# Moving the start addresses of SBUF tiles to multiples of 2 KB in a three-stage fp32 kernel

## The chip, the cores and the metric

The kernel runs on one core of a Trainium2 chip. The metric is the device time of one execution in microseconds, as the median of several runs. Beside it stands one profiled execution, from which every row below is taken.

## The reference, cut to what matters

Three stages follow each other. `q`, `k` and `v` are (8, 8, 576, 64), and positions attend to each other within chunks of 64 (`q_c`, `k_c`, `v_c`). The first network goes from 512 to 1024 columns twice, then to 1024 and back to 512; the second from 512 to 2048 and back. Everything is float32 and the result is (4608, 512).

```python
def _attn_ref(q, k, v):
    ...
    scores = scale * np.matmul(q_c, k_c.transpose(0, 1, 2, 4, 3))
    scores = scores - np.max(scores, axis=-1, keepdims=True)
    attn = np.exp(scores)
    attn = attn / (np.sum(attn, axis=-1, keepdims=True) + 1e-09)
    out = np.matmul(attn, v_c)
    ...

def _moe_ref(x, w1, w2, w3, w_out):
    a = x @ w1
    b = x @ w2
    h = a * b @ w3
    return (h @ w_out).astype(np.float32)

def _moe2_ref(x, w_in, w_out, alpha):
    h = x @ w_in
    g = np.maximum(h, 0.0) + alpha * np.minimum(h, 0.0)
    return (g @ w_out).astype(np.float32)
```

## The kernel before

**Arithmetic.** Each float32 operand of the large products is split into a high and a low half in a format that TensorE takes in one pass (`F32R`, four bytes an element), and a product is made of three matmuls: high with low, high with high, low with high (`PASSES`, line 24; `mm3`, lines 209 to 211). Each of these has 128x128 weights and 512 moving columns. The weights `w3` and `w_out` of the first network are multiplied with each other once at the start (`fold`, tile `wc`), so that the first network is two projections (`proj1`, tiles `a` and `b`), their product, and one projection through `wc` (`proj_wc`, accumulators `acc`). The second network is `proj2` and `proj_out`.

**Tiles in SBUF.** Four kinds matter here.
- *Granules* (`granule`, line 118): 32 slots of 4 KB in a partition, each two rows of 512 float32. They hold, one after another in time, `qk`, `v` and `e` of the attention, the weights `wa` and `wo`, the folded `wc`, and later the second network's `w2` (`w` in the profile). All matmuls but those of `fold` and `proj_out` take their weights from a granule; `fold` and `proj_out` take their moving rows from one.
- *x* (line 311, and line 382 for the second network, where the tile is `y`): two buffers of 16 KB, high and low half of 512 tokens. They are moving rows of `proj1` and `proj2`.
- *Halves of g* (`halves`, line 115, tag `gs`): three buffers of 4 KB. They are moving rows of `proj_wc` and weights of `proj_out`; `fold` takes its weights (`w3`) from them.
- *Temporaries*: `raw` (3 of 4 KB), `tmp` (8 of 2 KB: `m`, `p`, `a`, `g`, `y`, `o`), `pt` (4 KB), and small ones: `mx` and `sm` (64 bytes each, two buffers) and `warm` (4 bytes).

Pools are laid one after another in a partition and tags within a pool in the order of their first use, each rounded up to 32 bytes and no more. `const` holds `ident` (512 bytes) and `alpha_sb` (64 bytes); `gran` follows, then `work`, in which `warm` comes first, then `raw`, `tmp`, `mx`, `sm`, `pt`, `x` and `gs`. So the small tiles decide where the large ones behind them begin. Within a granule, in x and in the halves of g, a moving row begins a whole number of 2 KB behind the tile's start, and a block of weights a whole number of 512 bytes.

**Order.** Up to about 230 us the kernel follows a list of steps written out by hand (`STARTUP`), in which the attention of the first three blocks, the splitting of the weights and `proj1` are interleaved. Then come three blocks of `proj_wc`, from stored products (`g_dram`), then six blocks of `proj1`, `product` and `proj_wc` with the attention of later blocks between them, and then nine blocks of `proj2` and `proj_out`. All DMAs are issued from SyncE's queue. TensorE runs what the loops give it in order; the InOrder helper (lines 91 to 105) records every instruction of the three engines, so that all of them stand under line 100 in the profile, and tiles tell them apart.

Of the kernel before, what the change touches and what calls it, by code (L numbers as in the profile page):

```python
# [10 lines left out]
F32 = mybir.dt.float32  # L11
F32R = mybir.dt.float32r
AF = mybir.ActivationFunctionType
# [4 lines left out]
P = 128  # L18
# [41 lines left out]
def tile_attention_moe_moe(ctx: ExitStack, tc: tile.TileContext, qkv: bass.AP, w12: bass.AP,  # L60
# [16 lines left out]
    NU = NT // (2 * P)  # L77

    const = ctx.enter_context(tc.tile_pool(name="const", bufs=1))
    gran = ctx.enter_context(tc.tile_pool(name="gran", bufs=1))  # L80
    work = ctx.enter_context(tc.tile_pool(name="work", bufs=2))
    psum = ctx.enter_context(tc.tile_pool(name="psum", bufs=1, space=bass.MemoryType.PSUM))

    ident = const.tile([P, P], F32, name="ident")
    make_identity(nc, ident)
    alpha_sb = const.tile([P, NF2], F32, name="alpha_sb")
    g_dram = {(b, f): tc.dram_tile([P, TB], F32, name=f"g_dram{b}_{f}") for b in range(LEAD) for f in range(NF1)}
    y_dram = [tc.dram_tile([P, KD, TB], F32, name=f"y_dram{b}") for b in range(NB)]
    w2_dram = {(f, h): tc.dram_tile([P, 2, TB], F32, name=f"w2_dram{f}_{h}") for f in range(NF2) for h in range(2)}
# [15 lines left out]
    pe, act, dve = InOrder(nc.tensor), InOrder(nc.scalar), InOrder(nc.vector)  # L105
# [112 lines left out]
    un = {}  # L218
# [41 lines left out]
                                         start=True, stop=True)  # L260

    def attn_max(u):
        mx = un[u]["mx"] = work.tile([P, 2, 8], F32, tag="mx", name="mx")
        dve.tensor_reduce(out=mx, in_=un[u]["s"].rearrange("p h (a k) -> p h a k", k=D), axis=AX.X, op=ALU.max)
        dve.tensor_scalar_mul(mx, mx, -SCALE)

    def attn_exp(u, tiles=range(2)):
        mx, s, e = un[u]["mx"], un[u]["s"], un[u]["e"]
        if tiles[0] == 0:
            un[u]["sm"] = work.tile([P, 2, 4, 2], F32, tag="sm", name="sm")  # L270
        sm = un[u]["sm"]
        for j in tiles:
            for a in range(4):
                for h2 in range(2):
                    n, h = 4 * j + a, h2 ^ (a & 1 if u >= CROSS else 0)
                    act.activation(out=e[:, j, a, h], in_=s[:, h2, n * D:(n + 1) * D], func=AF.Exp,
                                         bias=mx[:, h2, n:n + 1], scale=SCALE, accum_out=sm[:, j, a, h:h + 1])
# [128 lines left out]

    act.activation(out=work.tile([P, 1], F32, tag="warm", name="warm", bufs=1), in_=ident[:, 0:1], func=AF.Exp)
    for u in range(4):  # L410
        unit_tiles(u)
    for load, n in ((load_qk, 0), (convert_load, 0), (load_qk, 1), (load_v, 0), (convert_load, 1), (load_v, 1),
# [6 lines left out]
    for step in STARTUP.split():  # L419
# [4 lines left out]
        elif kind in "ABCDE":  # L424
            {"A": convert_a, "B": convert_b, "C": convert_c, "D": convert_d, "E": convert_e}[kind](n)
        elif kind in "ST":
            {"S": attn_scores, "T": attn_transpose}[kind](n, lent.get(n, "att"))
        elif kind in "MXYPV":
            {"M": attn_max, "X": attn_exp, "Y": attn_softmax, "P": attn_copy, "V": attn_values}[kind](n)
        elif kind in "cd":  # L430
            attn_out(n, kind == "d")
        elif kind == "a":
            if sets % 2:
                pp = pair("p01", "ab")
                ab[tuple(rest)] = [pp[:, 0], pp[:, 1], None]
            else:
                ab[tuple(rest)] = [bank("a"), bank("b"), None]
            sets += 1
            proj1(*rest, 0, ab[tuple(rest)][0])
        elif kind == "k":  # L440
            a = ab[tuple(rest)][2] = tmp("a")
            act.copy(a, ab[tuple(rest)][0])
        elif kind == "b":
            proj1(*rest, 1, ab[tuple(rest)][1])
        elif kind == "m":
            _, ps, a = ab.pop(tuple(rest))
            product(*rest, a, ps)
        elif kind == "h":
            fold(*rest)
        elif kind in "sw":  # L450
            fold_split(n, kind == "w")
        elif kind == "g":
            load_g(*steps[n])


    def unit_steps(u, cut):


        def first():
            attn_scores(u)  # L460
            attn_max(u)
            attn_exp(u, range(1 if cut else 2))

        def second():
            if cut:
                attn_exp(u, range(1, 2))
            attn_softmax(u)
            if u + 1 < NU:
                load_unit(u + 1)

        def third():
            attn_transpose(u)
            attn_copy(u)

        def fourth():
            attn_values(u)
            attn_out(u, False)
            attn_out(u, True)
        return [first, second, third, fourth]
# [107 lines left out]
```

## Time and profile before

| | us |
|---|---|
| median of 3 runs | 1557.77 |
| lowest, highest | 1557.25, 1558.16 |
| the profiled execution | 1558.09 |
| its span, first to last instruction | 1556.3 |

The profiled execution is 0.3 us above the median, and 1.8 us of it lie outside the span. TensorE is busy for 98% of the span, VectorE for 51%, ScalarE for 27%; the chain of work that ended last is TensorE's for 95%. A busy TensorE is not TensorE at its peak, since matmuls are pipelined and each one's recorded length overlaps the next: what one costs is read from how far the starts of groups lie apart, not from the mean length.

### The profile page before, as it was taken

How to read it: one execution, taken by the hardware profiler on the slowest of the kernel's cores; microseconds unless marked ns; L12 is line 12 of the kernel's file. 1: busy time of each engine (PE TensorE's matmuls, PEld its weight loads, DVE VectorE, ACT ScalarE, POOL GpSimd, SP SyncE). 2: the span in 40 equal slices, each digit the busy share in tenths (PEclk: the TensorE clock that was granted, in tenths of full speed). 3: DMA queues.
4: the chain of work that ended last, by engine and by line, in shares of the span. 5: the costliest groups of instructions: out<-in, count | busy, mean ns of one | idle time of the engine just before them, and what ended most of it. 6: DMA issues, size and time to landing. Idle time of an engine off the chain costs nothing.

```text
span 1556.3 us, 21102 instructions
## 1 busy us (share of the span) xinstructions
PE 1530.3 (98%) x8688; PEld 1228.2 (79%) x8688; DVE 793.0 (51%) x1250; ACT 421.0 (27%) x1108; POOL 0.7 (0%) x6
## 2 busy tenths in 40 slices
PE   5999999999999999999999999999999999999998
PEld 5778877788888888888788888888888888888887
DVE  7988984376666663231434343443434344343433
ACT  6553335344444443321111111111111111111111
POOL 0000000000000000000000000000000000000000
PEclk9999999999999999999999999999999999999999
DMA  8544446354554544155301010010101000000000
GB/s 298 164 130 148 147 160 217 99 186 169 178 172 160 186 166 163 45 172 190 95 0 55 0 55 1 14 41 1 55 0 55 0 14 28 1 27 0 28 1 27
DMA packets 61712, 141.89 MB, mean 91 GB/s; under 512 B 6576, under 2 KB 20912, under 8 KB 61616
## 3 DMA queue, kind: packets, MB, share of 16 engines
q1 hardware_dynamic: 61616, 140.54, 27.1%
q8 instruction: 68, 1.11, 0.3%
q14 instruction: 28, 0.23, 0.0%
HBM read 98.57 MB, written 41.94 MB: 90 GB/s over the span
## 4 chain that ended last, share of the span: by engine, by line
PE 95%; DVE 2%; ACT 2%; DMA 1%; issue 0%; SPq 0%; ACTq 0%
PE acc L100 38%; PE b L100 24%; PE a L100 23%; PE ab L100 4%; PE wc L100 3%; PE pa L100 2%; PE sc L100 1%; ACT e L100 1%; DMA g<-g_dram 1%; DVE m L100 0%; DMA qk<-in_qkv 0%; DVE mx L100 0%; DVE p L100 0%; DVE e L100 0%; DVE x L100 0%
## 5 line engine op out<-in xcount | busy, mean ns | idle before, releaser
L100 PE MATMUL acc<-w,gs 128*128 128x512 f32 x1728 | 426.5, 396 | 0.0
L100 PEld LDWEIGHTS acc<-w,gs 128*128 128x128 f32 x1728 | 324.5, 188 | 78.8
L100 ACT CAST gs<-g 128x512 fp32r<-128x512 f32 x168 | 104.5, 622 | 683.2 <-DVE g L100 656.8
L100 PE MATMUL acc<-gs,wc 128*128 128x512 f32 x864 | 213.8, 398 | 2.1 <-DVE gs L100 2.1
L100 PE MATMUL b<-y,w 128*128 128x512 f32 x864 | 213.0, 395 | 0.0
L100 PE MATMUL a<-y,w 128*128 128x512 f32 x864 | 213.0, 395 | 0.0
L100 PEld LDWEIGHTS acc<-gs,wc 128*128 128x128 f32 x864 | 160.1, 187 | 43.4 <-DVE gs L100 3.4
L100 PEld LDWEIGHTS a<-y,w 128*128 128x128 f32 x864 | 162.0, 187 | 39.5
L100 PEld LDWEIGHTS b<-y,w 128*128 128x128 f32 x864 | 162.0, 187 | 39.5
L100 DVE TENSOR_TENSOR gs<-g,gs 128x512 fp32r<-128x512 f32 x168 | 116.3, 693 | 133.1 <-ACT gs L100 126.9
L100 PE MATMUL b<-x,wa 128*128 128x512 f32 x720 | 180.0, 398 | 0.1
L100 PE MATMUL a<-x,wa 128*128 128x512 f32 x720 | 178.1, 396 | 1.4 <-DVE x L100 1.4
L100 PEld LDWEIGHTS a<-x,wa 128*128 128x128 f32 x720 | 134.6, 187 | 34.5 <-DVE x L100 1.6
L100 PEld LDWEIGHTS b<-x,wa 128*128 128x128 f32 x720 | 133.3, 188 | 32.3 <-DVE wa L100 0.5
L100 DVE TENSOR_SCALAR g<-b,alpha_sb 128x512 f32<-128x512 f32 x72 | 54.0, 750 | 189.5 <-PE b L100 189.5
L100 DVE TENSOR_SCALAR g<-a,alpha_sb 128x512 f32<-128x512 f32 x72 | 54.0, 750 | 173.7 <-PE a L100 173.7
L100 DVE TENSOR_SCALAR m<-m 128x512 f32<-128x512 f32 (+1 forms) x144 | 60.9, 424 | 67.1 <-ACT m L100 65.7
L100 ACT ACTIVATE e<-sc,mx 128x64 f32<-128x64 f32 x288 | 85.7, 353 | 28.9 <-DVE mx L100 28.9
L100 DVE TENSOR_TENSOR a<-b,a 128x512 f32<-128x512 f32 x60 | 41.3, 689 | 93.3 <-PE b L100 82.5
L100 ACT COPY a<-a 128x512 f32<-128x512 f32 x60 | 35.9, 599 | 151.2 <-PE a L100 132.5
L100 PE MATMUL ab<-x,wa 128*128 128x512 f32 x288 | 71.1, 402 | 2.7 <-ACT a L100 2.7
L100 ACT ACTIVATION_READ_ACCUMULATOR e<-sc,mx 128x1 f32 x288 | 70.2, 247 | 0.0
(55 smaller groups left out, 982.2 us busy)
## 6 DMA issues: line engine op xcount, KB each, us to landing
qk<-in_qkv SPq DMA_DIRECT2D x36, 512.0 KB, 6.5
raw<-in_w2nd SPq DMA_DIRECT2D x32, 512.0 KB, 4.0
w_dram<-wm SPq DMA_DIRECT2D x32, 512.0 KB, 3.1
w<-w_dram SPq DMA_DIRECT2D x32, 512.0 KB, 3.3
y_dram<-y SPq DMA_DIRECT2D x36, 256.0 KB, 2.9
yraw<-y_dram SPq DMA_DIRECT2D x18, 512.0 KB, 4.2
out<-o SPq DMA_DIRECT2D x36, 256.0 KB, 2.1
raw<-in_w SPq DMA_DIRECT2D x16, 512.0 KB, 4.4
```

The lines of the kernel that those rows point to most:

```text
L100: ins = op(*args, **kw)
```

## The change

Only the places of tiles change. `mx` and `sm` move from the pool `work` to a pool of their own, `small`, with two buffers each as before; `warm` moves to `const`; and a tile of 1,056 bytes, `shift`, is laid down that nothing reads or writes. Starts in a partition, in bytes past a multiple of 2 KB:

| tiles | before | after |
|---|---|---|
| granules (32) | 704 | 0 |
| raw, tmp | 736 | 0 |
| pt, x, halves of g | 992 | 0 |
| mx, sm | 736 and 800, 864 and 928 | the same |
| ident | 128 | 128 |

Every engine gets the same instructions in the same order with the same waits on the same semaphores, before and after; only addresses differ. No tile shares a buffer with another than before, and the PSUM tiles stay where they are.

```diff
@@ -77,6 +77,8 @@
     const = ctx.enter_context(tc.tile_pool(name="const", bufs=1))
+    small = ctx.enter_context(tc.tile_pool(name="small", bufs=2))
+    shift = ctx.enter_context(tc.tile_pool(name="shift", bufs=1))
     gran = ctx.enter_context(tc.tile_pool(name="gran", bufs=1))
     work = ctx.enter_context(tc.tile_pool(name="work", bufs=2))
@@ -84,6 +86,8 @@
     alpha_sb = const.tile([P, NF2], F32, name="alpha_sb")
+
+    shift.tile([P, 264], F32, name="shift")
@@ -260,14 +264,14 @@
     def attn_max(u):
-        mx = un[u]["mx"] = work.tile([P, 2, 8], F32, tag="mx", name="mx")
+        mx = un[u]["mx"] = small.tile([P, 2, 8], F32, tag="mx", name="mx")
...
         if tiles[0] == 0:
-            un[u]["sm"] = work.tile([P, 2, 4, 2], F32, tag="sm", name="sm")
+            un[u]["sm"] = small.tile([P, 2, 4, 2], F32, tag="sm", name="sm")
@@ -406,7 +410,7 @@
-    act.activation(out=work.tile([P, 1], F32, tag="warm", name="warm", bufs=1), in_=ident[:, 0:1], func=AF.Exp)
+    act.activation(out=const.tile([P, 1], F32, name="warm"), in_=ident[:, 0:1], func=AF.Exp)
```

## Rows read from the trace of the kernel before

**Rows 1.** Page, part 1: busy us of each engine, share of the span, instructions.
```profile
PE 1530.3 (98%) x8688; PEld 1228.2 (79%) x8688; DVE 793.0 (51%) x1250; ACT 421.0 (27%) x1108; POOL 0.7 (0%) x6
```

**Rows 2.** Stretches: us, then PE, PEld, DVE, ACT, POOL, PEclk, DMA, GB/s.
```profile
20.00:290.00 270.00, 262.18 (x1876) 209.78 (x1877) 211.18 (x365) 120.05 (x340) 0.00 (x0) 0.99 0.52 166
290.00:742.00 452.00, 452.00 (x3209) 362.40 (x3207) 234.28 (x400) 173.30 (x520) 0.00 (x0) 1.00 0.47 158
742.00:1556.30 814.30, 809.66 (x3469) 650.68 (x3468) 336.55 (x468) 113.91 (x178) 0.00 (x0) 1.00 0.07 23
```

**Rows 3.** Groups by shape, TensorE: busy us, mean ns of one, idle before.
```profile
L100 PE MATMUL acc<-w,gs 128*128 128x512 f32 x1728 | 426.5, 396 | 0.0
L100 PEld LDWEIGHTS acc<-w,gs 128*128 128x128 f32 x1728 | 324.5, 188 | 78.8
L100 PE MATMUL acc<-gs,wc 128*128 128x512 f32 x864 | 213.8, 398 | 2.1 <-DVE gs L100 2.1
L100 PE MATMUL b<-y,w 128*128 128x512 f32 x864 | 213.0, 395 | 0.0
L100 PE MATMUL a<-y,w 128*128 128x512 f32 x864 | 213.0, 395 | 0.0
L100 PE MATMUL b<-x,wa 128*128 128x512 f32 x720 | 180.0, 398 | 0.1
L100 PE MATMUL a<-x,wa 128*128 128x512 f32 x720 | 178.1, 396 | 1.4 <-DVE x L100 1.4
...
L100 PE MATMUL ab<-x,wa 128*128 128x512 f32 x288 | 71.1, 402 | 2.7 <-ACT a L100 2.7
...
L100 PE MATMUL wc<-wo,w 128*128 128x512 f32 x192 | 45.6, 396 | 0.0
```

**Rows 4.** Chain of waits, whole span: start us, length us, engine, tile, count.
```profile
1.17 4.49 DMA qk<-in_qkv
...
162.87 11.20 PE wc L100 x48
...
188.08 5.60 PE ab L100 x24
```

**Rows 5.** Order of time, TensorE alone, 690 to 700 us.
```profile
691.65 2.96 PE L100 MATMUL a<-x,wa 128*128 128x512 f32 x12
694.45 2.96 PE L100 MATMUL b<-x,wa 128*128 128x512 f32 x12
```

**Rows 6.** Order of time, all engines, 900 to 912 us.
```profile
902.10 2.96 PE L100 MATMUL b<-y,w 128*128 128x512 f32 x12
904.67 2.75 PEld L100 LDWEIGHTS acc<-w,gs 128*128 128x128 f32 x12
904.90 2.96 PE L100 MATMUL acc<-w,gs 128*128 128x512 f32 x12
```

**Rows 7.** TensorE waits: us in total, times, longest.
```profile
PE sc L100 <- DMA qk<-in_qkv: 6.7, 3, 4.4
...
PE acc L100 <- DVE gs L100: 2.1, 3, 1.7
```

**Rows 8.** Chain of waits, 225 to 300 us: its two DMA pieces.
```profile
256.64 4.09 DMA g<-g_dram
...
282.31 5.21 DMA g<-g_dram
```

**Rows 9.** Groups by shape: VectorE on tiles of different starts.
```profile
L100 DVE TENSOR_TENSOR e<-e,sm 128x1024 f32<-128x1024 f32 x18 | 22.0, 1223 | 0.5
...
L100 DVE TENSOR_TENSOR x<-pa,x 128x1024 fp32r<-128x1024 f32 x18 | 21.9, 1223 | 9.1 <-ACT x L100 9.1
...
L100 DVE TENSOR_TENSOR y<-yraw,y 128x1024 fp32r<-128x1024 f32 x18 | 21.9, 1218 | 0.7 <-ACT y L100 0.7
```

**Rows 10.** Groups by shape: the two attention products on TensorE.
```profile
L100 PE MATMUL pa<-pt,v 64*64 64x64 f32 x1152 | 26.4, 227 | 4.1 <-ACT pt L100 4.1
...
L100 PE MATMUL sc<-qk 64*64 64x64 f32 x1152 | 23.2, 232 | 6.8 <-DMA qk<-in_qkv 6.7
```

## Prediction

> **What bounds the kernel now.** I read the shares of the engines first. TensorE is busy for 1530.3 of 1556.3 us [rows 1], so only 26.0 us of the span are not its own. The table of stretches says where: 7.8 us between 20 and 290 us, none between 290 and 742 us, 4.6 us after that [rows 2]; the other 13.6 us lie in the first 20 us, before the matmuls are under way. VectorE and ScalarE have slack everywhere after 290 us (234.28 and 173.30 us busy of 452) [rows 2]. The granted clock is 1.00 or 0.99 throughout [rows 2], that is the 2.4 GHz level.
>
> Then I ask what one long matmul costs. The list by shape has eight groups with 512 moving columns [rows 3]: 1728 + 3 x 864 + 2 x 720 + 288 + 192 = 6240 instructions. The mean length of one, 395 to 402 ns, is not its price, since records overlap. The starts of whole groups are: twelve from 691.65 to 694.45 us [rows 5], twelve from 902.10 to 904.90 us [rows 6], 24 in 5.60 us and 48 in 11.20 us on the chain [rows 4]. Each is 233.3 ns per matmul, which is 560 ticks at 2.4 GHz. 6240 x 233.3 ns = 1456 us, or 94% of the span. So the time is, nearly to the end, the number of long matmuls times one pace, and a change without instructions can move it in two ways only: through that pace, or through the few microseconds in which TensorE waits.
>
> Is the pace that of the weights? A load is recorded at 188 ns [rows 3], and the twelve loads of a group begin at 904.67 us, 0.23 us or one pace ahead of their matmuls at 904.90 us [rows 6]. It begins with the matmul before it and is over 45 ns before it is needed. So it is the moving side that takes 560 ticks for 512 columns: 48 ticks, 20.0 ns, more than one column a tick (512 / 2.4 = 213.3 ns). No row names the owner of these 20.0 ns, and they are what this change could reach.
>
> **The change part by part.** It removes, adds and moves no instruction and no wait. Four things could still change price.
>
> *The pace of long matmuls.* Before, a moving row of 2 KB starts at 704 past a multiple of 2 KB when it comes from a granule, and at 992 when it comes from x, y or the halves of g; it crosses one multiple of 2 KB either way. Weights are at the other of the two starts. The trace holds both pairings: in `ab` the rows come from x and the weights from a granule, and in `wc` rows come from a granule and weights from the halves. Both take 233.3 ns: 5.60 us for 24 and 11.20 us for 48 [rows 4]. One start is a multiple of 64 and the other is not, so any cost of a start that is off by a piece of 64 bytes or less would have set them apart; printed to 0.01 us, they differ by under 0.4 ns. What the trace can't show is a cost that every row pays, since no row in it starts on 128 bytes or more. The bounds: at best all of the 20.0 ns goes (6240 x 20.0 = 125 us), at worst something is added, which I price below as a rival (31 us). I take 0, by the nearest rows, the two pairings that agree.
>
> [...]
>
> *VectorE and ScalarE.* The same operation on 1024 elements took 1223 ns in granules at 704, 1223 ns from PSUM into x at 992, and 1218 ns from `raw` at 736 into y at 992 [rows 9]. So starts set these apart by 5 ns at most. Between 20 and 290 us VectorE and ScalarE run 365 + 340 instructions [rows 2]; even if the 365 of VectorE were all on the path, 5 ns each would be 1.8 us either way. I take 0. After 290 us TensorE's own work covers them, with no idle time up to 742 us [rows 2].
>
> *DMA.* Transfers end up on the chain at the start (4.49 us for the first `qk`) [rows 4] and twice at a reload of `g` (4.09 and 5.21 us) [rows 8]. TensorE itself waits 6.7 us for `qk`, and 2.1 us for the halves that follow such reloads [rows 7]. The two reloads move the same amount and differ by 1.12 us, so that much is ordinary scatter of one transfer; three of them give 3.4 us either way as a bound. I take 0, since bytes, packets and queue are the same.
>
> [...]
>
> *Small tiles.* `mx` and `sm` rotate over two buffers as before, so no wait is new, and `shift` has no instruction: 0.
>
> The sum is 0 against the profiled execution's 1558.09 us, and so against the median of 1557.77 us, which lies 0.3 us below it: **1557.8 us**. The bounds of VectorE and of DMA add to 5 us either way; I don't expect them together, and 0.2% of this time, about what a measurement of this kernel can tell from no change, is 3.1 us.
>
> **The rivals.**
>
> *The 20.0 ns are the price of unaligned rows (faster).* Every moving row now crosses a multiple of 2 KB, and afterwards none does. If a crossing or an off start of 128 bytes or more costs all 48 ticks, the time is 1557.8 - 125 = 1433 us; if it costs 16 of them, 6240 x 6.7 ns = 42 us go, and it is 1516 us. For it: the excess is the same for each matmul, and so is the crossing. Against it: two quite different starts have exactly one price, and a fixed cost of a matmul, or a rate for four-byte columns a little below the clock, explains the same 233.3 ns without addresses. [...]
>
> *Weights and rows now start in step (slower).* Before, rows and weights were 288 bytes apart past a multiple of 512, or 224 the other way; afterwards both begin at multiples of 512, and a load begins with the matmul before it, so both readers walk the same positions side by side. If they hinder each other, the moving row, which has no slack, pays at once, and the load decides nothing before it has used up its 45 ns. The nearest row is the attention's score product: q and k lie in one granule, exactly 2 KB apart, so in step already. It takes 232 ns in the mean, and the value product, whose operands lie 288 bytes out of step, 227 ns [rows 10]. 5 ns on each long matmul would be 31 us: 1589 us. Against it: the groups' busy times point the other way, 23.2 us in step and 26.4 us out of step for 1152 instructions each [rows 10].
>
> *The starts do not become multiples of 2 KB (same).* Then nothing changes at all: 1557.8 us. I count it with the forecast, since the places follow from the sizes of the tiles.
>
> **How the numbers follow.** No measurable change: 0.64, its own range 1554.7 to 1560.9 us. The pace falls by a tick or more: 0.20, between 1433 and 1555 us, most of it at the far end. Transfers and short operations together gain a little over 3.1 us: 0.04. Rows and weights in step: 0.09, up to 1589 us. Transfers or a wait that falls otherwise, a little over 3.1 us slower: 0.03. So faster 0.24, same 0.64, slower 0.12. The range takes in the forecast, the small gains and losses, and the slower rival up to its price, and leaves out the faster pace: 1547 to 1587 us, some 0.8 in all.
>
> **What would show it.** In the profile of the changed kernel, twelve long matmuls from group to group: 2.80 us says that addresses don't matter; 2.56 us says that rows were billed for their start, and anything above 2.80 us that the readers collide. The stretch from 290 to 742 us shows it alone, since TensorE has no wait there. The three DMA pieces on the chain should stay between 4 and 5.3 us. What would make the prediction wrong is a pace that answers to a start of 128 bytes or more, which no tile of the kernel before has.

## The result, and the profile after

The changed kernel takes 1518.74 us (median of 4 runs, 1517.43 to 1520.73) against 1557.51 us before in the same comparison. The ratio is 0.9753, with a 95% interval of 0.9736 to 0.9770: 38.8 us less, where no change was forecast. The time lies below the range. The profiled execution took 1519.76 us, with a span of 1518.0 us. One execution in this document ran at another clock, the profiled one of `pad32` below (2521.38 us at a granted clock of 0.56), so that `pad32` is read by the times of its other three.

The page's parts 1 and 4 after the change (busy us and instructions of each engine; shares of the chain that ended last):

```profile
PE 1492.4 (98%) x8688; PEld 1230.1 (81%) x8688; DVE 792.7 (52%) x1250; ACT 420.6 (28%) x1108; POOL 0.7 (0%) x6
...
PE 90%; DVE 5%; ACT 2%; DMA 1%; issue 1%; SPq 0%; DVEq 0%; ACTq 0%
```

Beside [rows 1], TensorE alone has changed: 37.9 us less for the same 8688 instructions. VectorE, ScalarE and the weight loads kept their times within 2 us. The groups by shape (busy us, mean ns of one, idle before; line 104 is the line that was 100) answer to [rows 3]:

```profile
L104 PE MATMUL acc<-w,gs 128*128 128x512 f32 x1728 | 414.8, 389 | 0.0
...
L104 PE MATMUL acc<-gs,wc 128*128 128x512 f32 x864 | 208.8, 393 | 1.6 <-DVE gs L104 1.4
L104 PE MATMUL b<-y,w 128*128 128x512 f32 x864 | 207.5, 389 | 0.0
...
L104 PE MATMUL wc<-wo,w 128*128 128x512 f32 x192 | 44.7, 390 | 0.2 <-DVE w L104 0.2
```

The pace itself stands in the order of time (start, length, engine, tile, count), which answers to [rows 6]:

```profile
890.55 2.88 PE L104 MATMUL acc<-w,gs 128*128 128x512 f32 x12
...
893.27 2.88 PE L104 MATMUL b<-y,w 128*128 128x512 f32 x12
...
895.99 2.88 PE L104 MATMUL acc<-w,gs 128*128 128x512 f32 x12
```

Twelve matmuls now take 2.72 us from start to start, where they took 2.80: 226.7 ns for one instead of 233.3, or 544 ticks instead of 560. A tick stands here for a 512th of 213.3 ns, which is half of the 426.7 ns that a matmul of 512 columns took where the granted clock was 0.50 (from 111.405 to 115.672 us in the trace of after, ten from start to start). The two groups that take their weights and their rows from opposite places have the same new pace, as they had the same old one.

Beside the pace little moved. VectorE's operations of [rows 9] read 1223, 1223 and 1219 ns, and TensorE's two waits of [rows 7] are 6.7 and 1.4 us, the second 0.7 us shorter than before:

```profile
L104 DVE TENSOR_TENSOR e<-e,sm 128x1024 f32<-128x1024 f32 x18 | 22.0, 1223 | 0.5
L104 DVE TENSOR_TENSOR y<-yraw,y 128x1024 fp32r<-128x1024 f32 x18 | 21.9, 1219 | 0.7 <-ACT y L104 0.7
L104 DVE TENSOR_TENSOR x<-pa,x 128x1024 fp32r<-128x1024 f32 x18 | 21.9, 1223 | 9.1 <-ACT x L104 9.1
```

```profile
PE sc L104 <- DMA qk<-in_qkv: 6.7, 2, 4.4
...
PE acc L104 <- DVE gs L104: 1.4, 2, 1.1
...
PE wc L104 <- DVE w L104: 0.2, 1, 0.2
```

The last of these lines is new. TensorE's share of the chain falls from 95 to 90%, since from 150 to 192 us the chain now runs through VectorE, which splits the weights; the wait of 0.2 us says that the two engines are about level there.

Of the DMA pieces on the chain one reload of `g` is left, with 4.63 us. At its start now stands another load, `raw<-in_w`, of 6.13 us, which is more than the 5.3 us that the prediction set as a bound; ScalarE's wait for that load is nearly the same, 5.4 us before and 5.6 us after.

**Where 3 us went.** 16 ticks less on 6240 matmuls are 41.6 us; the span fell by 38.3. Cut both executions at the start of the same group of `a` (before, then after; us, PE, PEld, DVE, ACT, POOL, PEclk, DMA, GB/s):

```profile
0.00:117.82 117.82, 98.34 (x1105) 79.91 (x1105) 99.44 (x173) 68.80 (x255) 0.70 (x6) 0.99 0.58 195
117.82:1556.30 1438.48, 1431.97 (x7584) 1148.30 (x7584) 693.57 (x1078) 352.17 (x853) 0.00 (x0) 1.00 0.25 83
```

```profile
0.00:117.62 117.62, 98.17 (x1105) 80.80 (x1105) 100.24 (x174) 68.55 (x255) 0.70 (x6) 0.97 0.58 197
117.62:1518.00 1400.38, 1394.19 (x7584) 1149.33 (x7584) 692.48 (x1077) 352.01 (x853) 0.00 (x0) 1.00 0.25 85
```

288 of the long matmuls lie ahead of the cut (they should have given 1.9 us and gave 0.2), 5952 behind it (39.7 us, of which 38.1 came). Ahead of the cut the chain says why (chain of waits after; start, length, what):

```profile
104.40 4.37 DMA raw<-in_wo
...
110.81 5.49 PE ab L104 x12
116.30 1.32 PE pa L104 x64
117.62 2.95 PE a L104 x12
```

TensorE comes to this place 1.35 us earlier (110.81 against 112.16 us) and waits there as long as before, 2.7 us, for a copy of `a` by ScalarE, behind which the chain now has a load of `raw`. But the granted clock has fallen to 0.50 for all twelve matmuls behind the wait (the columns as above):

```profile
110.80:116.00 5.20, 5.19 (x12) 3.81 (x12) 4.92 (x10) 2.34 (x4) 0.00 (x0) 0.50 0.20 72
```

In the trace of before it fell only at 113.56 us, when six of them had started. There the same group took 4.35 us on the chain instead of 5.49, so 1.1 us of the gain is given back. Of the 1.6 us missing behind the cut some 0.7 lie in the 22 groups that directly follow a piece of attention: a group of `b` behind the score product took 3.00 us on the chain before and takes 2.95 after, 0.05 us less and not 0.08. Why they gain less was not tried, and where the rest lies was not found.

### The profile page after: what moved, and what is told of

Its sections match the earlier page's. It is cut to its first block, busy times and chain, and to the rows that moved or that the text cites. A ratio compares the mean times of both kernels' runs of the same rounds, so it can differ in the third digit from the quotient of the medians.

```text
span 1518.0 us, 21102 instructions
## 1 busy us (share of the span) xinstructions
PE 1492.4 (98%) x8688; PEld 1230.1 (81%) x8688; DVE 792.7 (52%) x1250; ACT 420.6 (28%) x1108; POOL 0.7 (0%) x6
## 4 chain that ended last, share of the span: by engine, by line
PE 90%; DVE 5%; ACT 2%; DMA 1%; issue 1%; SPq 0%; DVEq 0%; ACTq 0%
PE acc L104 38%; PE b L104 23%; PE a L104 22%; PE ab L104 3%; DVE m L104 2%; PE pa L104 2%; PE wc L104 2%; ACT e L104 1%; DVE p L104 1%; PE sc L104 1%; DMA raw<-in_w 0%; DVE a L104 0%; DVE e L104 0%; DVE w L104 0%; DVE wa L104 0%
## 5 line engine op out<-in xcount | busy, mean ns | idle before, releaser
L104 PE MATMUL acc<-w,gs 128*128 128x512 f32 x1728 | 414.8, 389 | 0.0
L104 PE MATMUL acc<-gs,wc 128*128 128x512 f32 x864 | 208.8, 393 | 1.6 <-DVE gs L104 1.4
L104 PE MATMUL b<-y,w 128*128 128x512 f32 x864 | 207.5, 389 | 0.0
L104 PE MATMUL a<-y,w 128*128 128x512 f32 x864 | 207.5, 389 | 0.0
L104 PE MATMUL b<-x,wa 128*128 128x512 f32 x720 | 175.7, 393 | 0.1
L104 PE MATMUL a<-x,wa 128*128 128x512 f32 x720 | 173.5, 390 | 1.4 <-DVE x L104 1.4
```

The lines of the kernel that those rows point to most:

```text
L104: ins = op(*args, **kw)
```

## The experiments

**Which property of the places counts.** Four theories gave the same time for the change and were set apart by where the tiles start. Theory 1: rows or weights that start off a multiple of 64 bytes cost 16 ticks. Theory 2: a row that crosses a multiple of 2 KB does. Theory 3: rows must start on 128 bytes or more. Theory 4: what counts is not where rows and weights start but how far apart they are, modulo 512.

The kernel before, with x, the halves and the temporaries, all of which lie behind `warm`, moved by 32 bytes and the granules left in place (`pad32`):

```diff
-    act.activation(out=work.tile([P, 1], F32, tag="warm", name="warm", bufs=1), in_=ident[:, 0:1], func=AF.Exp)
+    act.activation(out=work.tile([P, 16], F32, tag="warm", name="warm", bufs=1)[:, 0:1], in_=ident[:, 0:1], func=AF.Exp)
```

> The kernel before with one edit: the tile warm takes 64 bytes instead of 32, so that what lies behind it in the pool moves by 32 bytes. Granules stay at 704 past a multiple of 2 KB; raw and tmp come to 768, x and the halves of g to 1024. Theory 1 (a long matmul pays 16 ticks, 6.7 ns, when either its rows or its weights start off a multiple of 64 bytes): granules at 704 were clean already, x and the halves now are too, so all eight groups fall from 2.80 to 2.72 us for twelve, and the time is that of the full change, 1518.7 us. Theory 2 (16 ticks for a row that crosses a multiple of 2 KB): every row still crosses one, 2.80 us and 1557.5 us. Theory 3 (rows must start on a multiple of 128 bytes or more): rows from x, y and the halves are clean (4320 matmuls, 28.8 us less), rows from granules at 704 are not (acc<-w,gs and wc, 1920 matmuls): 1529 us. Theory 4 (rows and weights must start in step modulo 512 bytes): 320 bytes out of step, 2.80 us and 1557.5 us.

1542.93 us (the middle one of three), a ratio of 0.9905 (0.9888 to 0.9921): a little over a third of the gain, and none of the four numbers. Only the time is used here; the distances come back below.

The changed kernel moved as a whole by 64 and by 32 bytes (`all64`, `all32`: the unused tile has 280 or 272 elements instead of 264):

```diff
-    shift.tile([P, 264], F32, name="shift")
+    shift.tile([P, 272], F32, name="shift")
```

> The changed kernel with its unused tile 64 bytes longer: granules, raw, tmp, pt, x and the halves all start at 64 past a multiple of 2 KB. Theory 1 (64 bytes): nothing is off, 2.72 us for twelve, 1518.7 us. Theory 2 (crossing 2 KB): every row crosses again, 2.80 us, 1557.5 us. Theory 3 (128 bytes or more): all rows are off, 2.80 us, 1557.5 us. Theory 4 (in step): still in step, 2.72 us, 1518.7 us.

> The changed kernel with its unused tile 32 bytes longer: granules, raw, tmp, pt, x and the halves all start at 32 past a multiple of 2 KB, so rows and weights of every long matmul are off a multiple of 64. Theory 1 has two forms. If each operand that is off costs 16 ticks, they add to 576 ticks: 2.88 us for twelve, 83 us over the changed kernel, 1602 us. If one is enough and the second is free, 2.80 us and 1557.5 us. Theories 2 and 3: 2.80 us, 1557.5 us. Theory 4 (in step): 2.72 us, 1518.7 us.

1517.97 us (ratio 0.9745, 0.9729 to 0.9762) and 1519.29 us (0.9754, 0.9740 to 0.9769): both as fast as the changed kernel, with every tile 32 bytes off a multiple of 64 in the second. In `all32`, order of time:

```profile
901.64 2.88 PE L104 MATMUL b<-y,w 128*128 128x512 f32 x12
904.36 2.88 PE L104 MATMUL acc<-w,gs 128*128 128x512 f32 x12
907.08 2.88 PE L104 MATMUL a<-y,w 128*128 128x512 f32 x12
```

2.72 us from group to group. Starts are free, multiples of 2 KB too, and theories 1 to 3 fall.

The kernel before, moved as a whole so that its granules alone come to a multiple of 2 KB (`gran_only`):

```diff
+    shift = ctx.enter_context(tc.tile_pool(name="shift", bufs=1))
     gran = ctx.enter_context(tc.tile_pool(name="gran", bufs=1))
...
+    shift.tile([P, 336], F32, name="shift")
```

> The kernel before with an unused tile of 1344 bytes ahead of the granules: granules start at a multiple of 2 KB, raw and tmp at 32, x and the halves of g at 288 past one; this is the granules' part of the change alone. Theory 1 (64 bytes, rows or weights): x and the halves are 32 off, and each long matmul has one operand there, so 2.80 us for twelve everywhere and 1557.5 us, no gain. Theories 2 and 3 (crossing 2 KB; 128 bytes or more, rows alone): rows from granules are clean, acc<-w,gs and wc fall to 2.72 us (1920 matmuls, 12.8 us), the rest stays: 1545 us. Theory 4 (in step): 288 bytes out of step as before, 1557.5 us.

1557.34 us, a ratio of 0.9999 (0.9990 to 1.0008), and in its order of time the old pace, 2.80 us:

```profile
901.06 2.96 PE L102 MATMUL b<-y,w 128*128 128x512 f32 x12
903.85 2.96 PE L102 MATMUL acc<-w,gs 128*128 128x512 f32 x12
906.66 2.96 PE L102 MATMUL a<-y,w 128*128 128x512 f32 x12
```

Together: places moved and distance kept, the pace stays (`gran_only` against before, `all32` and `all64` against after); distance changed, it changes. Of the four only theory 4 is left, and not as it was put: it had 1557.5 us for `pad32`, so there are more than two paces.

**How the pace depends on the distance.** Unused tiles ahead of x and of the halves of g put the rows of `proj1` and `proj2` (3456 matmuls: a, b, ab), of `proj_wc` (864: acc<-gs,wc) and the weights of `proj_out` and `fold` (1920: acc<-w,gs and wc) at distances of choice from the granules. Each of these runs, and of all that follow, is one execution beside one of the kernel before; the 13 executions of that kernel beside the four runs above lie between 1556.69 and 1558.85 us, so that differences under some 2 us say nothing here.

```diff
+            if b == 0:
+                work.tile([P, 64], F32, tag="pad_x", name="pad_x", bufs=1)
             x_t[b] = work.tile([P, 2, KD, TB], F32R, tag="x", name="x", bufs=2)
...
+        if not pads:
+            pads.append(work.tile([P, 72], F32, tag="pad_g", name="pad_g", bufs=1))
         return work.tile([P, 2, TB], F32R, tag="gs", name=name, bufs=3)
```

> The changed kernel with two unused tiles, one ahead of x and one ahead of the halves of g: granules stay at 0 past a multiple of 512 bytes, x comes to 256, the halves to 32. So the rows of proj1 and proj2 (3456 matmuls: a, b, ab) start 256 bytes behind their weights modulo 512; those of proj_wc (864) 32 behind; those of proj_out and fold (1920) 32 ahead. All starts at 32 past a multiple of 2 KB left the pace as fast as all starts at 0, so a start by itself is free and theories 1 to 3 have fallen; the distance is what is asked here. Theory 4a (only a distance of 0 modulo 512 is fast): 2.80 us for twelve everywhere, 1557 us. Theory 4b (the distance counts modulo 128: 0 is fast at 544 ticks, 64 lies between, 32 and 96 are slow at 560): a, b and ab at 2.72 us, the rest at 2.80 us, which costs 2784 x 6.7 ns = 18.5 us over 1518.7: 1537 us.

1537.63 us, as theory 4b said, beside 1557.96 us for the kernel before:

```profile
901.18 2.89 PE L104 MATMUL b<-y,w 128*128 128x512 f32 x12
903.91 2.96 PE L104 MATMUL acc<-w,gs 128*128 128x512 f32 x12
906.71 2.89 PE L104 MATMUL a<-y,w 128*128 128x512 f32 x12
```

The group of b, 256 bytes apart, takes 2.73 us, and that of acc, 32 bytes apart, 2.80 us, alternating in one kernel. Two distances in one execution have two paces, so nothing that the whole kernel shares can be the cause.

> As before, with x at 32 and the halves at 64 past a multiple of 512, granules at 0. Theory 4a: 2.80 us for twelve everywhere, 1557 us. Theory 4b: a, b and ab (distance 32) slow at 2.80 us; acc and wc (64 behind or ahead) between, at about 2.77 us, the pace that the kernel with 320 between its tiles shows by its time: 1551 us. Theory 1, had it stood: a, b, ab at 2.80 us, the rest at 2.72 us, 1542 us.

1551.96 us, where theory 4b had 1551, but by luck, as its groups show:

```profile
905.94 2.96 PE L104 MATMUL acc<-w,gs 128*128 128x512 f32 x12
908.74 2.95 PE L104 MATMUL b<-y,w 128*128 128x512 f32 x12
911.53 2.96 PE L104 MATMUL acc<-w,gs 128*128 128x512 f32 x12
```

The group of acc<-w,gs, 64 ahead, should have taken 2.77 us and takes 2.80, so a distance and its mirror image are not the same; the time comes from acc<-gs,wc, 64 behind, at 2.746 us, and from b and a, which take 2.79 us.

> As before, with x at 64 and the halves at 128 past a multiple of 512, granules at 0. Theory 4a: 2.80 us for twelve everywhere, 1557 us. Theory 4b: a, b and ab (64) between, at about 2.77 us; acc and wc (128 behind or ahead) fast, 2.72 us: 1532 us.

1545.43 us, not 1532: at 128 the pace is the old one.

```profile
902.40 2.96 PE L104 MATMUL acc<-w,gs 128*128 128x512 f32 x12
905.20 2.93 PE L104 MATMUL b<-y,w 128*128 128x512 f32 x12
907.97 2.96 PE L104 MATMUL acc<-w,gs 128*128 128x512 f32 x12
```

> As before, with x at 128 and the halves at 192 past a multiple of 512, granules at 0. Theory 4a: 2.80 us for twelve everywhere, 1557 us. Theory 4b: a, b and ab (128) fast, 2.72 us; acc and wc (192 behind or ahead) between, at about 2.77 us: 1529 us. The wc and acc<-w,gs groups of this run have the distance 320 that a, b and ab had in the run with 320 between its tiles.

1549.48 us, not 1529. Theory 4b falls with these two. In the second network 0 and 256 agree within 0.01 us (2.72 and 2.73), and so do 64 and 320 (2.76 and, here as acc<-w,gs, 2.77), so the distance counts modulo 256 as far as was tried. `pad32` had 64 modulo 256 for rows of x and of the halves: 3456 x 3.0 ns for a, b and ab (2.764 us for twelve) and 864 x 4.5 ns for acc<-gs,wc (2.746 us in `x32_gs64`) are 14.3 us, and it gained 14.3.

Then finer steps, with x and the halves moved inside larger tiles. The tiles grow by 256 bytes, so from one buffer to the next these distances are the same only modulo 256:

```diff
-        return work.tile([P, 2, TB], F32R, tag="gs", name=name, bufs=3)
+        return work.tile([P, 2 * TB + 64], F32R, tag="gs", name=name, bufs=3)[:, 12:12 + 2 * TB].rearrange("p (s t) -> p s t", s=2)
```

> The changed kernel with x starting 4 bytes and the halves of g 8 bytes past their multiple of 256 (by room of 256 bytes more in each tile), granules at 0. If the distance counts in pieces of 16 bytes, 4 and 8 bytes lie in the same piece as 0: 2.72 us for twelve everywhere, 1519 us. If each byte counts: 2.79 us or so, 1555 us. The groups acc<-w,gs have the weights 8 bytes ahead, which is the piece before: they may fall off alone, 11.5 us.

1562.7 us, which neither theory had, 6 us slower than the kernel before (1556.72 us). Four bytes of distance turn the best pace into the slowest that was read, 2.84 us:

```profile
900.47 3.00 PE L104 MATMUL a<-y,w 128*128 128x512 f32 x12
903.31 2.93 PE L104 MATMUL acc<-w,gs 128*128 128x512 f32 x12
906.07 3.00 PE L104 MATMUL b<-y,w 128*128 128x512 f32 x12
```

> As before with x at 16 and the halves at 48: distances 16 (a, b, ab), 48 (acc<-gs,wc) and 208 modulo 256 (acc<-w,gs, wc). If 0 is a single good place: 2.79 us for twelve everywhere, 1556 us. If the pace rises with the distance from 0: a, b and ab between 2.72 and 2.79 us, some 1540 us. If odd multiples of 16 are better than 0: under 2.72 us.

> As before with x at 80 and the halves at 112: distances 80, 112 and 144. If 0 and 64 are the only places below 2.79 us: 2.79 us everywhere, 1556 us. If places near 64 share its pace: a, b and ab at about 2.765 us, 1544 us. If odd multiples of 16 are better than 0: under 2.72 us.

> As before with x at 240 and the halves at 176: distances 240, 176 and 80 (the last also a, b and ab of the run with x at 80, so that the two roles can be compared). If 0 is a single good place: 2.79 us everywhere, 1556 us. If places 16 bytes from 0 are partly good on this side: a, b and ab below 2.79 us.

1549.73, 1544.85 and 1555.80 us. The first is none of its forecasts. The second is the one by which places near 64 share its pace (a and b at 2.77 us). The third has the time of "0 is a single good place" by luck: its groups were to take 2.79 us, but a and b take 2.81 and acc<-w,gs 2.76. The paces of all these runs, as starts of one group to the next in us for twelve (the median over the groups), by the distance of rows behind weights modulo 256:

| distance | us for twelve | read in |
|---|---|---|
| 0 | 2.72 | after, all64, all32; 2.73 at 256 |
| 4 | 2.84 | x4_gs8 (a, b) |
| 8 | 2.78 | x4_gs8 (acc<-gs,wc) |
| 16 | 2.78 | x16_gs48 |
| 32 | 2.79 to 2.80 | x32_gs64, gran_only, x256_gs32 |
| 48 | 2.80 | x16_gs48 |
| 64 | 2.76, 2.77, 2.75 | x64_gs128, x128_gs192 (acc<-w,gs), x32_gs64 (acc<-gs,wc) |
| 80 | 2.77, 2.76 | x80_gs112, x240_gs176 (acc<-w,gs) |
| 112 | 2.77 | x80_gs112 |
| 128 | 2.80, 2.80 | x128_gs192, x64_gs128 (acc<-w,gs) |
| 144 | 2.79 | x80_gs112 |
| 176, 192, 208, 224 | 2.80, 2.80, 2.79, 2.80 | x240_gs176, x128_gs192, x16_gs48, before |
| 240 | 2.81, 2.80 to 2.84 | x240_gs176 (a, b from y; from x) |
| 248 | 2.77 | x4_gs8 (acc<-w,gs) |

64, 80 and 128 were run with the granule as weights and with the granule as rows and gave the same pace within 0.02 us, so it matters little which pool holds the weights. But the distance doesn't fix the pace alone. In `x240_gs176`, two groups of `b` of one block, with the same buffer of x and so the same distance of 240:

```profile
651.85 3.00 PE L104 MATMUL b<-x,wa 128*128 128x512 f32 x12
654.69 2.94 PE L104 MATMUL acc<-gs,wc 128*128 128x512 f32 x12
...
670.89 2.96 PE L104 MATMUL b<-x,wa 128*128 128x512 f32 x12
673.69 2.96 PE L104 MATMUL acc<-gs,wc 128*128 128x512 f32 x12
```

The first takes 2.84 us and the second 2.80, with the value product of the attention, at 664.09 us, between them. So what ran ahead may have a part in the pace, which was not tried, and a number of the table belongs to the stream in which it was read, often in turn with another distance. Zero is the best place of those run, and no rule for the rest was found.

**Who owns the excess.** Two theories for the 48 (or 32) ticks over 512. Theory 5: each load of weights, read beside the rows, costs its matmul that much. Theory 6: the rows come at that rate whatever is loaded. Columns in two halves, with twice the loads (`split_before`, `split_after`):

```diff
-        for k in range(KD):
-            mm3(ps, lambda s: w[:, s, k], lambda m: y[:, m, k], k == 0, k == KD - 1)
+        for c in (slice(0, TB // 2), slice(TB // 2, TB)) if f % 2 else (slice(0, TB),):
+            for k in range(KD):
+                mm3(ps[:, c], lambda s: w[:, s, k], lambda m: y[:, m, k, c], k == 0, k == KD - 1)
```

> The kernel before; in proj2, at every odd f (tile b), each matmul of 512 columns is made as two of 256 columns, the first half of the columns for all twelve pairs of operands and then the second half, so 24 matmuls and 24 weight loads where there were 12. The places are those of before (288 bytes between rows and weights modulo 512). Theory 5 (rows and a load of weights that is read at the same time hold each other up, so the excess of 48 ticks belongs to each load): 256 + 48 = 304 ticks a matmul, 24 in 3.04 us. Theory 6 (the rows themselves come at 35 ticks for 32 columns, whatever is loaded): 280 ticks, 24 in 2.80 us. Nothing but the pace of b (from y) is asked; the other groups stay at 2.80 us for twelve. Time by theory 5: 72 groups x 0.24 us more, 1575 us; by theory 6: 1558 us.

> The same edit on the changed kernel (distance 0). Theory 5 (the excess, here 32 ticks, belongs to each load): 288 ticks, 24 in 2.88 us, and 72 x 0.16 us more, 1530 us. Theory 6 (34 ticks for 32 columns): 272 ticks, 24 in 2.72 us, 1519 us.

1557.61 and 1531.39 us. In the first, 24 matmuls of half the columns take the 2.80 us of twelve whole ones; in the second 2.87 us instead of 2.72:

```profile
901.62 2.96 PE L100 MATMUL b<-y,w 128*128 128x256 f32 x24
904.42 2.96 PE L100 MATMUL acc<-w,gs 128*128 128x512 f32 x12
```

```profile
905.70 3.04 PE L104 MATMUL b<-y,w 128*128 128x256 f32 x24
908.57 2.91 PE L104 MATMUL acc<-w,gs 128*128 128x512 f32 x12
```

So at the old distance theory 6 holds to the digit, and at distance 0 theory 5 does. With 256 columns the order of the two distances turns round: 116.7 ns a matmul at the old one, 119.6 ns at 0. Then loads of half the columns (`half_before`, `half_after`):

```diff
+        if f % 2:
+            for k in range(KD):
+                mm3(ps[0:P // 2], lambda s: w[:, s, k, 0:P // 2], lambda m: y[:, m, k], k == 0, k == KD - 1)
```

> The kernel before; in proj2, at every odd f (tile b), twelve matmuls are added behind the twelve, which compute the first 64 rows of the result a second time, with 64 columns of weights instead of 128 and the same 512 columns of rows. [...] It adds 72 x 12 matmuls, some 200 us. Theory 5 (the excess belongs to the load): half of 48 ticks, so 536 ticks and 2.68 us for the twelve short loads. Theory 6 (rate of the rows alone): 560 ticks, 2.80 us, as with full loads.

> The same edit on the changed kernel. Theory 5: half of 32 ticks, 528 ticks, 2.64 us for the twelve short loads. Theory 6: 544 ticks, 2.72 us.

```profile
912.31 5.75 PE L100 MATMUL b<-y,w 128*128 128x512 f32 x24
917.89 2.96 PE L100 MATMUL acc<-w,gs 128*128 128x512 f32 x12
```

```profile
907.02 5.64 PE L104 MATMUL b<-y,w 128*128 128x512 f32 x24
912.50 2.88 PE L104 MATMUL acc<-w,gs 128*128 128x512 f32 x12
```

The two runs take 1757.1 and 1718.14 us. Twelve whole loads and twelve short ones take 5.58 us at the old distance (2.80 and so 2.78), and 5.48 us at distance 0 (2.72 and so 2.76). By the records a short load takes 134 to 135 ns and a whole one 188, so it is shorter, though not by half. It leaves the excess nearly as it was at the old distance, and at distance 0 it makes the matmul slower. So theory 5 falls in its simple form, and theory 6 doesn't explain distance 0. Nor would a fixed cost of each matmul: it explains the split at distance 0, but not that a shorter load costs more. No run has rows without loads, so what the rows alone would take is not known. What is shown is that full loads at distance 0 beside rows of 512 columns run 16 ticks faster than at 288, and that with 256 columns this gain turns into a loss.

## Why the prediction was wrong

**What bounds the kernel** was right: one pace times 6240, with all waits and all other engines beside it. The gain came through that pace alone, and the two ways in which a change without instructions can move the time were the right two.

**The term for the pace** is the step that failed. "I take 0, by the nearest rows, the two pairings that agree": the term measured 6.7 ns for each long matmul, 41.6 us for all of them, of which 38.8 us came. The pairings of [rows 4] were taken for two different places. For starts they are; for the distance they are rows 288 bytes behind the weights and rows 288 ahead (32 and 224 modulo 256, both at 2.80 us before), and the 0 of the changed kernel is in neither. `gran_only` shows that the same distance at other starts has the same pace. Rows that agree say nothing on a value that none of them has. They were weak on starts too: each pairing has one operand at 992, off a multiple of 64, so a cost of any operand that is off would have been the same in both. That starts are free was shown only by `all32`, and the prediction's own condition for being wrong, a pace that answers to a start of 128 bytes or more, is not what happened.

**The owner of the 20.0 ns.** The prediction gave the 560 ticks to the moving side, since a load is over 45 ns before it is needed, and left open why, with a fixed cost of a matmul and a rate below the clock as the harmless readings. The first half was too quick: the pace answers to the place of the rows against that of the weights, so both sides have a part in it. One row of the trace of before would have narrowed the second. The mean clock of 0.99 between 20 and 290 us [rows 2] hides a stretch at 0.50 from 113.56 us on, after TensorE had waited 2.7 us up to 112.16 us (tile `ab` alone; stretch, PE, PEld, DVE, ACT, PEclk, DMA, GB/s):

```profile
113.74:115.88 2.14, 2.14 (x6) 1.65 (x5) 0.00 (x0) 0.00 (x0) 0.50 0.00 0
```

Five matmuls begin in these 2.14 us: 427 ns each. At distance 0 it is the same: of the twelve matmuls at 0.50 in the trace of after, from 110.81 us on, the second to the twelfth also start 427 ns apart. With as many ticks as at the clock of 1.00 it would be 467 ns at the old distance and 453 ns at 0. So at 0.50 the distance doesn't show. The prediction's 2.4 GHz can be read there alone, as a rate: 512 columns in 427 ns are 1.2 columns a ns at 0.50, and twice that at 1.00. That the whole excess of 20.0 ns is gone at 0.50 is an estimate from the same 427 ns, which takes them to have nothing over. A difference that is there at one clock and not at the other is not simply added to each matmul, in nanoseconds or in ticks. It fits something that can't keep up at the full clock, and such a thing may depend on where operands lie; that is an argument, not a measurement.

**The faster rival** had the right size, with its middle case of 16 ticks at 1516 us (measured: 16 ticks, 1518.74 us), and the wrong cause: `all32` has unaligned rows and all of the gain. It had 0.20 of the chance. The best pace of any run here is 226.7 ns.

**The slower rival** had the right quantity, rows and weights in step, with the wrong sign. Its own rows spoke against it ([rows 10]: 23.2 us in step, 26.4 us out of step) and it was priced by the mean length of one, 5 ns, which is not what an instruction costs. Nor were those rows near ones. The change brought the value product in step too (modulo 256), and it kept its 26.4 us, so its small matmuls, 64 by 64, don't show the effect:

```profile
L104 PE MATMUL pa<-pt,v 64*64 64x64 f32 x1152 | 26.4, 228 | 4.1 <-ACT pt L104 4.1
```

The long ones do: 2.72 us in `all32`, 2.80 us in `gran_only`. That the reads of rows and of weights meet is the plain reading, but it was not seen directly.

**The other terms** held. VectorE and ScalarE at 0: 792.7 us against 793.0, and 420.6 against 421.0. DMA at 0: TensorE's wait for `qk` is 6.7 us in both. Small tiles at 0: no wait for them is new.

**The range** left the faster pace out, since it was given 0.20, and the signs to look for had 2.56 and 2.80 us for twelve but nothing between. The chance was too low because the two agreeing pairings were counted as evidence on addresses as such. At its upper end the range stops at 1587 us, 2 us short of the slower rival's price that it was to take in.

What stays open: why 0 modulo 256 is better, why 4 bytes are worst, why a stream can keep one of two paces at one distance, and why a short load or short rows lose the gain at 0. The map of distances was read for this shape alone, 128 columns of weights and 512 of rows.

## What to carry to other kernels

When one pace times a count is the time, look for a stretch at a lower granted clock and compare the two: here a matmul took 427 ns at 0.50 and 233.3 ns at 1.00, less than twice, so the pace was not one number of ticks, and places moved it. For a stream of four-byte matmuls, try the same start modulo 512 bytes for the pools of rows and of weights (one unused tile does it; here 2.72 against 2.80 us for twelve), and measure, since matmuls of 256 columns were faster at the old distance (116.7 against 119.6 ns). And before two rows are called evidence that a variable doesn't matter, write down its value in both, and the value that the change will give it. When a time comes out as forecast, look at the groups before the theory is believed: `x32_gs64` and `x240_gs176` had the time and not the paces.

## What the runs showed of the hardware that was not expected

At a granted clock of 1.00 a matmul of 512 four-byte columns with 128 columns of weights took 226.7 to 236.7 ns in this kernel (544 to 568 ticks), by the distance in bytes between its two operands in a partition; at 0.50 it took 427 ns, at distance 288 as at 0. The distance did not fix the pace alone: in `x240_gs176` groups of b at one distance took 2.84 or 2.80 us for twelve, with the value product of the attention between them. A distance of 4 bytes, which pools that round to 32 bytes can't give, took 2.84 us for twelve in `x4_gs8`, against 2.72 us at a distance of 0.
